# Three weight loads of a fused state-space and gated feed-forward kernel moved to other places in their DMA queues

## The chip, the cores and the metric

The kernel runs on one core of one Trainium2 chip. The metric is the device time of one execution in microseconds (us), the median of several runs. One further execution was recorded by the hardware profiler, and its trace is what the views below answer from. Times inside it count from the start of the span, the first recorded instruction to the last.

The engines are called PE (TensorE, matmul), PEld (its weight loads), DVE (VectorE), ACT (ScalarE), POOL (GpSimd) and SP (SyncE). A name with a q behind it (SPq, ACTq) is that engine's instruction queue issuing a DMA.

## The reference

```
xn = layernorm(x)                                     # x: 2048 tokens x 512
# A: diagonal complex state-space layer, 512 states
Bu = xn @ B_bar.T                                     # B_bar from B_re, B_im, Lambda, dt
h[t] = Lam_bar * h[t-1] + Bu[t]                       # complex scan over the 2048 tokens
yA = 2 * Re(h @ C.T) + xn * Dskip                     # C = C_re + i C_im
# B: gated feed-forward, 1376 hidden columns
yB = (silu(xn @ w_gate) * (xn @ w_up)) @ w_down
out = x + yA + yB                                     # bf16
```

## The kernel before

The 2048 tokens go in four chunks of 512. Everything on TensorE is a matmul with 512 moving columns, four of them (one for each 128 of the 512 inputs) into one PSUM bank. For each chunk there is a B projection (`bproj_tile`, 8 tiles: 4 groups of states for the real and 4 for the imaginary part, L370), a gate/up pass (`gateup_tile`: 10 full column blocks of gate and of up, L445, and a mixed last block, L503) and later the output matmuls. ScalarE takes each bank out of PSUM (L372 for the B projection, L464 and L465 for gate and up, L506 and L507 for the last block). VectorE makes the rotations, scans and products of the state-space part. There are 8 PSUM banks, given out in turn by one pool.

The instructions of each engine stand in the order in which the Python code emits them. VectorE work comes out of a backlog, a few pieces after each group of matmuls (`pump`). The order around the change is

1. gate/up columns 0 to 6 of chunk 0, for which the weights came in groups 0 to 2,
2. the B projection of chunk 0, first the four real tiles, then the four imaginary ones,
3. the rest of chunk 0's gate/up pass: blocks 7 to 9 from group 3 (384 columns of `w_gate` in `wg_g[3]`, 384 of `w_up` in `wu_g[3]`), and the last block from `w_last`,
4. the B projection of chunk 1, then its gate/up pass, and so on.

The loads are issued by hand. SP's queue carries the token tiles (`xall`), the weight groups, the transposed loads of `B_re` and `B_im` into `BT` (four DMA transposes each, L138), the transposes of the normalized tokens of chunk 1 (L249, one for each 128 tokens), then by `load_late` the tokens of chunks 2 and 3 (L156) and `w_down` in two halves (`wd_sb`, L159), and then the eight transposed loads of `C_re` and `C_im` (`CT`, L862). `load_mid` is called before step 1, `load_late` just before step 3.

`wu_last` is a small tile: the last block's first 64 up columns. It is loaded from ScalarE's queue (L155) at the head of `load_late`, and is used by `up_halves` (L492), after chunk 0's output matmuls.

A DMA that SP or ScalarE issues tells of its landing through one of eight semaphores, which the framework gives to these DMAs in turn, in the order in which the code issues them. A DMA whose semaphore is still in use by an earlier one is issued only after that one has landed: the wait stands in the instruction stream of the engine that issues it.

Of the kernel before, what the change touches and what calls it, by code (L numbers as in the profile page):

```python
# [23 lines left out]
def kernel(  # L24
# [17 lines left out]
    nc = tc.nc  # L42
# [9 lines left out]
    KD = D // 128  # L52
    HK = KD // 2
# [6 lines left out]
    LA, LB = 32, 64  # L60
    FL = (FT - 1) * 128
# [20 lines left out]
    wg_v = B_w_gate.rearrange("(k p) f -> p k f", p=128)  # L82
    wu_v = B_w_up.rearrange("(k p) f -> p k f", p=128)
# [6 lines left out]
    wg_g, wu_g = [], []  # L90
# [5 lines left out]
    wu_last = const.tile([128, KD, LB], BF16, name="wu_last")  # L96
# [14 lines left out]
    def load_w1(q, tiles, view, gi):  # L111
        a, b = fgroups[gi]
        q.dma_start(out=tiles[gi][:], in_=view[:, :, a * 128:min(F, b * 128)])
# [23 lines left out]
    def load_bt(part, k):  # L137
        nc.sync.dma_start_transpose(out=BT[:, part, k, :], in_=(A_B_re, A_B_im)[part][:, k * 128:(k + 1) * 128])  # L138
# [4 lines left out]
    def load_mid():  # L143
        nc.sync.dma_start(out=xall[:, TPC:2 * TPC, :], in_=x_v[:, TPC:2 * TPC, :])
        for k in range(HK, KD):
            load_bt(0, k)
        for k in range(KD):
            load_bt(1, k)
        load_w1(nc.sync, wg_g, wg_v, 3)
        load_w1(nc.sync, wu_g, wu_v, 3)  # L150
        nc.sync.dma_start(out=w_last[:, :, 0:LB + LA], in_=wg_v[:, :, FL:F])
        nc.sync.dma_start(out=w_last[:, :, LB + LA:128], in_=wu_v[:, :, FL + LB:F])

    def load_late():
        nc.scalar.dma_start(out=wu_last[:], in_=wu_v[:, :, FL:FL + LB])  # L155
        nc.sync.dma_start(out=xall[:, 2 * TPC:NT, :], in_=x_v[:, 2 * TPC:NT, :])  # L156
        wd_v = B_w_down[0:FL, :].rearrange("(k p) d -> p k d", p=128)
        for a, b in ((0, FT // 2), (FT // 2, FT - 1)):
            nc.sync.dma_start(out=wd_sb[:, a:b, :], in_=wd_v[:, a:b, :])  # L159
# [351 lines left out]
    def gateup_tile(c, fi):  # L511
        if fi == FT - 1:
            return gateup_last(c)
        psg = bank()
        gu_mm(psg, wg_g, c, fi, 0, CW)
        psu = bank()
        gu_mm(psu, wu_g, c, fi, 0, CW)
        gu_out(c, fi, psg, psu)
# [113 lines left out]
    def pump(us):  # L632

        owed[0] += us
        while backlog and owed[0] >= backlog[0][0] * 0.5:
            step()
        if not backlog:
            owed[0] = 0.0

    def multiply(keep):  # L640

        while len(products) > keep:
            products.pop(0)()
            owed[0] -= 0.65
# [75 lines left out]
    norm_dve(3)  # L720
    xT_dma(3)
    load_mid()
    head_mm(0, 2, 3, range(0, HK), range(H))
    head_mm(1, 2, 3, range(0, HK), range(H))
# [116 lines left out]
    for part in range(2):  # L841
        for q in range(NQ):
# [10 lines left out]
           ["ln2"] * len(norm2) + ["ln3"] * (len(stats3) + len(norm3)))  # L853
    queue("cf", c_ops())
    load_late()
    for fi in range(G0, FT):
        gateup_tile(0, fi)
        pump(GU)
        multiply(1)
    for part, src in enumerate((A_C_re, A_C_im)):  # L860
        for q in range(NQ):
            nc.sync.dma_start_transpose(out=CT[:, part, q, :], in_=src[:, q * 128:(q + 1) * 128])  # L862
# [50 lines left out]
```

## Time and profile before

| | |
|---|---|
| median of 3 runs | 178.35 us (178.32 to 178.7) |
| the profiled execution's own time | 178.76 us |
| its span | 177.0 us |
| PE busy | 173.5 us, 98% |
| DVE busy | 153.9 us, 87% |
| ACT busy | 95.3 us, 54% |
| DMA queue of SP (q1) | 11.51 MB, 27.3% of 16 engines' span |
| DMA queue of ACT (q10) | 0.62 MB, 1.7% |

In the views, a line of the chain or the timeline starts with the start time and the duration in us. For a DMA in a queue's timeline, this duration is the time that the issue takes in the queue, not the transfer. A line of DMA issues ends with the time in us from the issue to the landing. "x4" means four instructions in one line.

### The profile page before, as it was taken

How to read it: one execution, taken by the hardware profiler on the slowest of the kernel's cores; microseconds unless marked ns; L12 is line 12 of the kernel's file. 1: busy time of each engine (PE TensorE's matmuls, PEld its weight loads, DVE VectorE, ACT ScalarE, POOL GpSimd, SP SyncE). 2: the span in 40 equal slices, each digit the busy share in tenths (PEclk: the TensorE clock that was granted, in tenths of full speed). 3: DMA queues.
4: the chain of work that ended last, by engine and by line, in shares of the span. 5: the costliest groups of instructions: out<-in, count | busy, mean ns of one | idle time of the engine just before them, and what ended most of it. 6: DMA issues, size and time to landing. Idle time of an engine off the chain costs nothing.

```text
span 177.0 us, 2607 instructions
## 1 busy us (share of the span) xinstructions
PE 173.5 (98%) x955; PEld 84.1 (48%) x955; DVE 153.9 (87%) x233; ACT 95.3 (54%) x174; POOL 51.8 (29%) x86
## 2 busy tenths in 40 slices
PE   8999999999999999999999999999999999999993
PEld 2977644444444444444444444444444444444443
DVE  3779999999999997999999999999999999971033
ACT  3477898867797679613666661053866610001300
POOL 6050120002300210029997040058476500001410
PEclk9999999999999999999999999999999999999999
DMA  5998497996440014900000020019699200000652
GB/s 169 306 167 204 91 257 80 305 305 129 89 87 6 0 36 82 355 5 17 17 19 17 0 82 11 0 20 129 88 147 189 46 2 0 0 4 0 63 98 76
DMA packets 31292, 16.36 MB, mean 92 GB/s; under 512 B 20208, under 2 KB 31088, under 8 KB 31248
## 3 DMA queue, kind: packets, MB, share of 16 engines
q1 hardware_dynamic: 24704, 11.51, 27.3%
q0 software_dynamic: 5184, 4.07, 15.9%
q10 hardware_dynamic: 1392, 0.62, 1.7%
q8 instruction: 7, 0.11, 0.3%
q14 instruction: 5, 0.04, 0.1%
HBM read 8.33 MB, written 5.24 MB: 77 GB/s over the span
## 4 chain that ended last, share of the span: by engine, by line
PE 98%; DVE 0%; issue 0%
PE ps L445 35%; PE ps L594 16%; PE ps L370 16%; PE ps L556 10%; PE ps L582 10%; PE ps L683 2%; PE ps L660 2%; PE ps L503 2%; PE ps L759 2%; PE ps L545 2%; PE ps L492 1%; PE ps L235 1%; DVE res L599 0%; PE ps L265 0%
## 5 line engine op out<-in xcount | busy, mean ns | idle before, releaser
L445 PE MATMUL ps<-xnT,wg 128*128 128x512 bf16 (+1 forms) x148 | 36.6, 373 | 0.0
L445 PE MATMUL ps<-xnT,wu 128*128 128x512 bf16 (+1 forms) x148 | 36.6, 373 | 0.0
L412 DVE TENSOR_TENSOR_SCAN g<-r_t,car,u 128x512 bf16<-128x512 f32 x24 | 28.8, 1263 | 0.0
L370 PE MATMUL ps<-xnT,BT 128*128 128x512 bf16 x128 | 28.3, 379 | 0.0
L594 PE MATMUL ps<-CF,wt 128*128 128x512 bf16 (+2 forms) x144 | 28.2, 356 | 0.0
L464 ACT ACTIVATE guT<-ps 128x512 bf16<-128x512 f32 (+1 forms) x40 | 23.5, 587 | 6.7 <-PE ps L445 6.0
L465 ACT CAST u<-ps 128x512 bf16<-128x512 f32 (+1 forms) x40 | 23.0, 575 | 6.9 <-PE ps L445 6.6
L607 ACT CAST res<-ps 128x512 bf16<-128x512 f32 x12 | 6.7, 590 | 36.0 <-PE ps L594 26.8
L445 PEld LDWEIGHTS <-wu 128*128 128x128 bf16 x148 | 14.5, 98 | 16.6
L187 POOL DMA_DIRECT2D gu_rows<-ul x36 | 17.6, 499 | 15.8 <-DVE ul L480 15.8
L445 PEld LDWEIGHTS <-wg 128*128 128x128 bf16 x148 | 14.4, 98 | 16.5
L608 POOL DMA_DIRECT2D out_dram<-res x12 | 10.5, 1220 | 37.4 <-ACT res L607 37.2
L372 ACT CAST u<-ps 128x512 bf16<-128x512 f32 x32 | 18.2, 586 | 6.0 <-PE ps L370 5.9
L594 PEld LDWEIGHTS <-wt 128*128 128x128 bf16 x144 | 13.3, 98 | 15.0 <-issue 1.3
L370 PEld LDWEIGHTS <-BT 128*128 128x128 bf16 x128 | 12.5, 98 | 14.8
L212 POOL TENSOR_TENSOR rstd<-ve,neg_half 128x2 f32<-128x2 f32 (+1 forms) x4 | 5.7, 1418 | 44.4 <-DVE ve L211 44.4
L582 PE MATMUL ps<-wd_sb,guT 128*128 128x512 bf16 x80 | 17.6, 379 | 0.0
L556 PE MATMUL ps<-wd_sb,guT 128*128 128x512 bf16 x80 | 17.4, 379 | 0.0
L460 DVE TENSOR_TENSOR guT<-guT,u 128x1024 bf16<-128x1024 bf16 x20 | 13.4, 677 | 0.0
L582 PEld LDWEIGHTS <-guT 128*128 128x128 bf16 x80 | 7.8, 98 | 9.4
L556 PEld LDWEIGHTS <-guT 128*128 128x128 bf16 x80 | 7.8, 98 | 9.4
L203 DVE BATCH_NORM_STATS2 stats<-xall 128x6 f32<-128x512 bf16 x14 | 9.5, 679 | 1.9 <-DMA xall<-in_A_x_dram 1.8
(120 smaller groups left out, 200.8 us busy)
## 6 DMA issues: line engine op xcount, KB each, us to landing
out_dram<-in_A_x_dram SPq DMA_DIRECT2D x1, 1536.0 KB, 6.8
out_dram<-res POOLq DMA_DIRECT2D x12, 128.0 KB, 3.6
out_dram<-xall POOLq DMA_DIRECT2D x3, 512.0 KB, 7.4
wd_sb<-in_B_w_down_dram SPq DMA_DIRECT2D x2, 640.0 KB, 7.7
xall<-in_A_x_dram SPq DMA_DIRECT2D x1, 1024.0 KB, 5.9
gu_rows<-ul POOLq DMA_DIRECT2D x36, 8.0 KB, 1.6
wg<-in_B_w_gate_dram SPq DMA_DIRECT2D x1, 512.0 KB, 5.0
wu<-in_B_w_up_dram SPq DMA_DIRECT2D x1, 512.0 KB, 6.0
```

The costliest lines, as they stand in the source:

```text
L187: nc.gpsimd.dma_start(out=gu_rows[c][i * RT:(i + 1) * RT, p, :], in_=product[p * RT:(p + 1) * RT, i * 128:(i + 1) * 128])
L370: nc.tensor.matmul(ps[:], lhsT=BT[:, part, k, q * 128:(q + 1) * 128], rhs=xnT[:, k, c * CW:(c + 1) * CW], start=(k == 0), stop=(k == KD - 1))
L372: nc.scalar.copy(out=u_tiles[c][:, part, q, :], in_=ps[:])
L412: V.tensor_tensor_scan(out=g()[:, part, q, :], data0=r_t[:, q:q + 1].to_broadcast([128, CW]), data1=u_tiles[c][:, part, q, :], initial=ini ...
L445: nc.tensor.matmul(ps[:fs, lo:hi], lhsT=wslice(groups, fi, k), rhs=xnT[:, k, c * CW + lo:c * CW + hi], start=(k == 0), stop=(k == KD - 1))
L460: products.append(lambda: V.tensor_tensor(out=g, in0=g, in1=u, op=ALU.mult))
L464: nc.scalar.activation(out=gu_tile(c)[:, fi, 0:hi], in_=psg[:, 0:hi], func=ACT.Silu)
L465: nc.scalar.copy(out=u_tile(c, fi)[:, fi % 2, 0:hi], in_=psu[:, 0:hi])
L556: nc.tensor.matmul(o[:], lhsT=gu_tiles[k][:, fi, i * 128:(i + 1) * 128], rhs=wd_sb[:, fi, :], start=(fi == 0), stop=False)
L582: nc.tensor.matmul(o[:], lhsT=gu_tiles[c][:, fi, i * 128:(i + 1) * 128], rhs=wd_sb[:, fi, lo:hi], start=(fi == 0), stop=False)
L594: nc.tensor.matmul(o, lhsT=w_tiles[c][:, part, q, i * 128:(i + 1) * 128], rhs=CF[:, part, q, lo:hi], start=(fresh and part == 0 and q == 0 ...
L608: nc.gpsimd.dma_start(out=out_v[:, n, :], in_=res[:], accum_op=ALU.add)
```

## The change

The gate weights' last group is issued between the second and the third imaginary B transpose, where it stood behind the fourth. The up weights' last group stays behind the fourth. The load of `wu_last` goes from the head of `load_late`, ahead of the remaining gate/up blocks of chunk 0, to behind them. It stays in ScalarE's queue. No arithmetic is changed, and each engine's compute instructions keep their order.

```diff
@@ load_mid
         for k in range(HK, KD):
             load_bt(0, k)
-        for k in range(KD):
-            load_bt(1, k)
-        load_w1(nc.sync, wg_g, wg_v, 3)
-        load_w1(nc.sync, wu_g, wu_v, 3)
+        for groups, view, ks in ((wg_g, wg_v, range(0, HK)), (wu_g, wu_v, range(HK, KD))):
+            for k in ks:
+                load_bt(1, k)
+            load_w1(nc.sync, groups, view, 3)
         nc.sync.dma_start(out=w_last[:, :, 0:LB + LA], in_=wg_v[:, :, FL:F])
         nc.sync.dma_start(out=w_last[:, :, LB + LA:128], in_=wu_v[:, :, FL + LB:F])
 
     def load_late():
-        nc.scalar.dma_start(out=wu_last[:], in_=wu_v[:, :, FL:FL + LB])
         nc.sync.dma_start(out=xall[:, 2 * TPC:NT, :], in_=x_v[:, 2 * TPC:NT, :])
...
@@ behind load_late()
     for fi in range(G0, FT):
         gateup_tile(0, fi)
         pump(GU)
         multiply(1)
+    nc.scalar.dma_start(out=wu_last[:], in_=wu_v[:, :, FL:FL + LB])
     for part, src in enumerate((A_C_re, A_C_im)):
         for q in range(NQ):
             nc.sync.dma_start_transpose(out=CT[:, part, q, :], in_=src[:, q * 128:(q + 1) * 128])
```

## The prediction

> **What bounds the kernel now.** I read the page first, then the chain of waits in order of time, then the queues of SP and ACT around the moved loads.
>
> ```profile
> PE 173.5 (98%) x955; PEld 84.1 (48%) x955; DVE 153.9 (87%) x233; ACT 95.3 (54%) x174; POOL 51.8 (29%) x86
> ...
> 25.92 5.18 PE ps L445 x24
> 31.10 0.86 PE ps L503 x4
> 31.96 6.91 PE ps L370 x32
> 38.87 0.86 PE ps L503 x4
> ...
> 174.27 0.02 issue
> 174.29 0.29 DVE res L599
> ```
>
> TensorE bounds everything. The chain is a row of matmul groups without a hole: 24 gate/up matmuls take 5.18 us (0.216 each), the 32 of chunk 1's B projection 6.91 (0.216 each). So no load that the change moves is waited for now, and there is nothing to gain where they are used: if the first gate matmul of the last group waited, the 25.92 line would be longer than 24 x 0.216 = 5.18. On the other side PE has no slack, so any hole that the change makes is paid in full at the end. The whole question is whether it makes one.
>
> **The gate group between the transposes.** Rows of SP's queue and of landings, before:
>
> ```profile
> 10.97 0.59 SPq L144 DMA_DIRECT2D xall<-in_A_x_dram  x1
> 11.60 1.75 SPq L138 DMA_TRANSPOSE BT<-in_A_B_re_dram  x1
> 13.39 1.27 SPq L138 DMA_TRANSPOSE BT<-in_A_B_re_dram  x1
> 17.32 1.26 SPq L138 DMA_TRANSPOSE BT<-in_A_B_im_dram  x1
> 18.62 1.26 SPq L138 DMA_TRANSPOSE BT<-in_A_B_im_dram  x1
> 19.93 0.58 SPq L113 DMA_DIRECT2D wg<-in_B_w_gate_dram  x1
> ...
> xall<-in_A_x_dram SPq DMA_DIRECT2D x1, 512.0 KB, 4.4
> BT<-in_A_B_re_dram SPq DMA_TRANSPOSE x1, 4.2
> BT<-in_A_B_re_dram SPq DMA_TRANSPOSE x1, 3.5
> BT<-in_A_B_im_dram SPq DMA_TRANSPOSE x1, 2.7
> wg<-in_B_w_gate_dram SPq DMA_DIRECT2D x1, 384.0 KB, 4.0
> ...
> 18.85 7.07 PE L370 MATMUL ps<-xnT,BT 128*128 128x512 bf16 x32
> ```
>
> The fourth imaginary transpose is issued at 18.62 and lands 2.7 later, at 21.3. It is the weight of the 20th matmul of chunk 0's B projection, which starts at 18.85 + 19 x 0.216 = 22.95: 1.6 us of slack. After the change the gate group takes the slot at 17.32, and the third and fourth transposes queue behind it. The trace has this pattern once: 512 KB of `xall` issued at 10.97 landed at 15.4, the transpose behind it (its issue stretched to 1.75) landed 4.2 after 11.60, at 15.8, and the next one 3.5 after 13.39, at 16.9. So the two land 0.4 and 1.5 behind the copy. The gate group, landing 4.0 after 17.32, is there at 21.3, the third transpose at 21.7 (its matmul starts at 22.74) and the fourth at 22.8, for a need at 22.95. By the same pattern the fourth is issued at 17.32 + 0.62 + 1.79 = 19.73 and with 2.7 lands at 22.4, with 3.5 at 23.2. I take no stall; the bounds are 0 and 0.3 us. What hides a small stall is the larger one below: a PE that is late at 23 has as much less to wait at 39.
>
> The issues behind are pushed by about half a microsecond, to an end of 22.7, still ahead of the next transpose at 23.14, so SP's later work does not move from this. The up group keeps its place. No gain anywhere: nothing waited for these groups.
>
> **`wu_last` out of the way of SP's queue.** Here the move does something:
>
> ```profile
> 23.14 1.22 SPq L249 DMA_TRANSPOSE xnT<-xall  x1
> 24.45 1.21 SPq L249 DMA_TRANSPOSE xnT<-xall  x1
> 25.76 2.48 SPq L249 DMA_TRANSPOSE xnT<-xall  x1
> 28.32 1.29 SPq L249 DMA_TRANSPOSE xnT<-xall  x1
> 29.67 0.57 SPq L156 DMA_DIRECT2D xall<-in_A_x_dram  x1
> 30.91 0.68 SPq L159 DMA_DIRECT2D wd_sb<-in_B_w_down_dram  x1
> ...
> 27.50:28.50 1.00, 1.00 (x6) 0.48 (x5) 0.91 (x2) 0.81 (x2) 0.00 (x0) 1.00 1.49 34
> ...
> q10 hardware_dynamic: 53, 0.01, 80.7%
> ...
> wd_sb<-in_B_w_down_dram SPq DMA_DIRECT2D x1, 640.0 KB, 8.3
> ```
>
> The four transposes of chunk 1 are issued back to back. Three take 1.21 to 1.29 us, the third takes 2.48, and it is the one beside which ACT issues `wu_last` (25.97, below). In the stage 27.5 to 28.5 the DMA engines are counted as full (1.49, the two queues on top of each other) and move 34 GB/s; 80.7% of it is 53 packets of q10, ACT's queue, which is `wu_last`. The small load and the transposes block each other. With `wu_last` gone from there, the third issue should take 1.22, and all behind it on SP comes 2.48 - 1.22 = 1.26 us earlier: the second half of `w_down` is issued at 29.65 instead of 30.91. It landed at 30.91 + 8.3 = 39.2; now at 37.95. By itself this gives nothing, since PE waits for none of these.
>
> **`wu_last` in its new place.** In the built program its issue stands in ACT's stream right behind the two evictions of the last block, ahead of the eight of chunk 1's B projection, and it has the semaphore that the second `w_down` half uses just before it:
>
> ```
> SP   30  DMACopy wd_sb<-in_B_w_down_dram 128x5x512     [waits DMAHW6]
> ACT  44  TensorCopy ul<-ps 32x512
> ACT  45  DMACopy wu_last<-in_B_w_up_dram 128x4x64      [waits DMAHW6]
> ```
>
> SP 30 waits for the third count of this semaphore and makes the fourth; ACT 45 waits for the fourth, so for the landing of `w_down`. Before, it waited for `w_last`, which had landed by then. This is an added wait, and queued behind it on ACT are all evictions of PSUM.
>
> ```profile
> 24.32 2.23 ACT L372 CAST u<-ps 128x512 bf16<-128x512 f32 x4
> 25.97 0.41 ACTq L155 DMA_DIRECT2D wu_last<-in_B_w_up_dram  x1
> ...
> 32.61 0.58 ACT L507 CAST ul<-ps 32x512 bf16<-32x512 f32 x1
> 33.21 1.11 ACT L372 CAST u<-ps 128x512 bf16<-128x512 f32 x2
> ...
> 38.71 1.03 PE L503 MATMUL ps<-xnT,w_last 128*128 128x512 bf16 x4
> ...
> 45.54 0.81 ACT L225 ACTIVATE xall<-xall,nb,rstd 128x512 bf16<-128x512 bf16 x1 [1.73 <-DVE nb L215]
> ...
> 138.75 2.45 POOL L187 DMA_DIRECT2D gu_rows<-gu_last  x5 [2.26 <-DMA out_dram<-xall]
> ```
>
> That an issue held back for an earlier landing stops its engine's stream is what the POOL line shows: 2.26 us idle ahead of five small DMAs, ended by the landing of a store. ACT reaches its new wait at 32.61 + 0.58 = 33.2 and stands until 37.95. Meanwhile PE goes on: bank by bank the eight tiles of chunk 1's B projection fill all 8 banks, the last being the one that L507 released at 33.2. The next bank needed is the first tile's, for the last block of chunk 1, now started at 38.71. It comes free when ACT has issued the DMA (0.41, the 25.97 line) and copied that tile (0.58, as the L507 line and the L372 lines): 37.95 + 0.41 + 0.58 = 38.94. Three hand-overs (landing to issue, issue to copy, copy to matmul) add some 0.05 each, by the gaps between SP's issues (23.14 + 1.22 to 24.45 is 0.09): 39.09. **PE waits 39.09 - 38.71 = 0.38 us.** Bounds: without hand-overs and a landing 0.25 earlier, 0; with a landing 0.4 later, 0.8.
>
> [...] Had the wait sat in the DMA queue, ACT would pass it and the sum would be 0.
>
> After that ACT has eight tiles to catch up, about 0.48 each when they lie ready (two in 1.11 us, with the second's own 0.58, are at most 0.53 apart), against 0.86 us of PE for each bank. It reaches chunk 1's second gate/up pair at about 45.3, where it idled 1.73 us before 45.54, so the lag is gone and no second hole follows. DVE's products of chunk 1 come after that.
>
> The load itself now runs beside the `CT` transposes, which it may slow by the same 1.3 us; neither is needed soon:
>
> ```profile
> L353 ACT ACTIVATE cm<-CT,c2re x4: 715/716/734, 65.7 to 70.8; 128x512 f32<-128x512 bf16 x4
> L492 PE MATMUL ps<-xnT,wu_last x16: 379/379/403, 72.5 to 74.0; 128*64 128x512 bf16 x16
> ```
>
> **Sum.** 0 for the groups, 0 for SP's relief by itself, +0.38 for the hole near 38.9. The profiled execution goes from a span of 177.0 to 177.38 and from 178.76 to 179.14; against the median, which is 0.41 below that execution, 178.35 + 0.38, about **178.75 us**. A difference of 0.2% (0.36 us) is about what a measurement of this kernel can tell from no change, so the forecast lies close to that line.
>
> **Rivals.**
>
> *SP's relief doesn't come, or only in part.* If the third transpose's 2.48 us has another cause (the loads in flight ahead of it), `w_down` lands at 39.2 as before, the first tile's bank is free at 39.2 + 0.99 + 0.15 = 40.34, and PE waits 1.63: 179.98 us. For it: other issues right behind large copies were stretched too (the 1.75 at 11.60). Against: here no large copy was issued just before, two transposes in between took 1.22 and 1.21, and the q10 row names the culprit. A partial form: the DMA engines gave `wu_last` some 0.8 x 1 us between 27.5 and 28.5; if the transposes got only half of it back, the hole is about 1.2, 179.6 us. [...] Chance of this rival 0.14.
>
> *The fourth imaginary transpose is late by more than the hole hides.* From a landing of 23.4 on, the stall at 23 exceeds 0.4 and sets the end; at 0.5 beyond the bound of 23.2, it would be 0.75: 179.1 us. For it: the slack of 1.6 shrinks to 0.15. Against: the gate group is a quarter smaller than the copy of the pattern. Chance 0.05.
>
> *No hole, and a little faster.* From a landing of 37.55 on, 0.4 earlier than worked out, ACT's wait is covered by the eight banks, and PE never stops. What then can be gained is what PE loses elsewhere; `wu_last`'s first matmuls at 72.5 have one of 403 ns against 379, so some hundredths: 178.3 us. To gain over 0.2% the work outside PE's chain (0.8 us ahead of it, 2.7 behind 174.27) would have to shrink, which nothing in the change touches. Chance of a gain over 0.2%: 0.03.
>
> **How the numbers follow.** The forecast (a hole of 0 to 0.9 at 39) has 0.76; a little over half of it, 0.42, lies above 0.36, the rest, 0.34, below. Slower by over 0.2%: 0.42 + 0.14 + 0.05 = 0.61. Faster: 0.03. Within 0.2%: 0.36, with 0.02 for what I have not named. The range goes from no hole (178.3) to the first rival in full (180.0).
>
> **What would show it.** In the profile after: the chain of waits has a hole, or an ACT copy of L371, between the B projection of chunk 1 and its last block; SP's third chunk-1 transpose takes about 1.2; `w_down`'s second half is issued near 29.65; ACT idles from 33.2 for about 5 us and ends it by a DMA. I am wrong if ACT's evictions go on through 33 to 38, if the third transpose still takes 2.5, or if PE stands near 23.

## The result, and the profile after

The changed kernel takes 179.58 us (median of 6 runs, 179.25 to 180.01) against 178.33 us for the kernel before (6 runs, 178.23 to 178.7): slower by 1.25 us, ratio 1.0071 with a 95% interval of 1.0054 to 1.0087. It was forecast slower at 178.75, in a range of 178.3 to 180.0. The direction and the added wait came as forecast; the size is over three times the +0.38 of the sum. The trace below is of an execution of 180.01 us, the longest of the six.

The chain of waits after (start, duration, what; compute lines of after stand one lower than before, L371 is the eviction of the B projection that was L372) is no longer PE alone:

```profile
27.68 0.85 SPq L248
28.58 0.57 SPq L155
29.21 0.57 SPq L158
29.82 8.98 DMA wd_sb<-in_B_w_down_dram
38.83 0.41 ACTq L859
39.28 0.59 ACT u L371
39.91 1.02 PE ps L502 x4
40.94 17.27 PE ps L444 x80
...
175.49 0.29 DVE res L598
```

It is to be read upwards from 39.91: the last block of chunk 1 (L502) waited for an eviction, the eviction for ACT's issue of `wu_last` (L859), and the issue for the landing of the second `w_down` half, which SP had issued at 29.82. From there on PE runs without a hole, as before.

ACT's timeline shows the stop from the other side, and the list of waits gives it a name:

```profile
32.01 0.58 ACT L506 CAST ul<-ps 32x512 bf16<-32x512 f32 x1
38.83 0.41 ACTq L859 DMA_DIRECT2D wu_last<-in_B_w_up_dram  x1
39.28 4.01 ACT L371 CAST u<-ps 128x512 bf16<-128x512 f32 x8 [6.69 <-DMA wd_sb<-in_B_w_down_dram]
...
46.29 0.84 ACT L224 ACTIVATE xall<-xall,nb,rstd 128x512 bf16<-128x512 bf16 x1
...
54.79 0.59 ACT L464 CAST u<-ps 128x512 bf16<-128x512 f32 x1 [0.19 <-PE ps L444]
...
31.21 7.07 PE L369 MATMUL ps<-xnT,BT 128*128 128x512 bf16 x32
39.91 1.02 PE L502 MATMUL ps<-xnT,w_last 128*128 128x512 bf16 x4 [1.64 <-ACT u L371]
```

ACT computes nothing for 6.69 us, then makes the eight evictions of the B projection in one go (4.01 us, about 0.5 each). It waits for PE again only at 54.79; until then it works without a pause. PE's wait is 1.64 us by this view.

That is more than the 1.2 us by which the profiled span grew (177.0 to 178.2), because in this execution PE had come to the B projection of chunk 0 earlier:

```profile
18.26 7.07 PE L369 MATMUL ps<-xnT,BT 128*128 128x512 bf16 x32
```

It was 18.85 before, 0.59 later. The view counts PE's wait from the modelled end of the last matmul, which overlaps the start of the next. From start to start the delay is 39.91 - (31.21 + 6.91) = 1.79 us, with 6.91 us for 32 matmuls, and 1.79 - 0.59 = 1.20. In the changed kernel most of such a lead is lost, since the landing sets the time at which PE goes on: a second profile of it, further down, has PE there at 18.88 and a span only 0.2 longer. From the restart to the end of the span it is 178.2 - 39.91 = 138.3 us; before, from the same matmul, 177.0 - 38.71 = 138.3. So the span after is the landing, plus 1.11 us to PE's restart, plus 138.3, and the price of the change is the restart at 39.91 against the 38.71 of before: 1.20.

### The profile page after: what moved, and what is told of

Its sections match the earlier page's. It is cut to its first block, busy times and chain, and to the rows that moved or that the text cites. A ratio compares the mean times of both kernels' runs of the same rounds, so it can differ in the third digit from the quotient of the medians.

```text
span 178.2 us, 2607 instructions
## 1 busy us (share of the span) xinstructions
PE 173.0 (97%) x955; PEld 83.5 (47%) x955; DVE 153.8 (86%) x233; ACT 94.4 (53%) x174; POOL 51.9 (29%) x86
## 3 DMA queue, kind: packets, MB, share of 16 engines
q1 hardware_dynamic: 24704, 11.51, 27.6%
q10 hardware_dynamic: 1392, 0.62, 1.2%
## 4 chain that ended last, share of the span: by engine, by line
PE 80%; DVE 10%; DMA 5%; SPq 1%; issue 1%; POOL 1%; ACT 0%; ACTq 0%; DVEq 0%; POOLq 0%
PE ps L444 29%; PE ps L593 16%; PE ps L555 10%; PE ps L581 10%; PE ps L369 8%; DMA wd_sb<-in_B_w_down_dram 5%; PE ps L659 2%; DVE pm L304 2%; PE ps L544 2%; PE ps L502 2%; DVE pm L303 2%; DVE stats L202 1%; PE ps L682 1%; PE ps L491 1%; DVE guT L459 1%; DVE pm L295 1%
## 5 line engine op out<-in xcount | busy, mean ns | idle before, releaser
L593 PE MATMUL ps<-CF,wt 128*128 128x512 bf16 (+2 forms) x144 | 28.2, 356 | 0.0
L371 ACT CAST u<-ps 128x512 bf16<-128x512 f32 x32 | 17.7, 598 | 11.0 <-DMA wd_sb<-in_B_w_down_dram 6.7
L607 POOL DMA_DIRECT2D out_dram<-res x12 | 10.6, 1223 | 37.7 <-ACT res L606 37.6
```

The costliest lines, as they stand in the source:

```text
L371: nc.scalar.copy(out=u_tiles[c][:, part, q, :], in_=ps[:])
L593: nc.tensor.matmul(o, lhsT=w_tiles[c][:, part, q, i * 128:(i + 1) * 128], rhs=CF[:, part, q, lo:hi], start=(fresh and part == 0 and q == 0 ...
```

## The experiments

The theory: ACT stands at the moved issue until `w_down`'s second half has landed, and PE runs out of free banks; all of the loss is there. The rivals: the gate group between the transposes costs the time, or the small load does, by its place or traffic, whatever it waits for. Each kernel below was timed against runs of the kernel before on the same chip (178.46 us for the first four, 178.41 for the next four).

**One part of the change at a time.** The change moves two loads, the gate group (by which two B transposes go later) and `wu_last`. First only the move of `wu_last`:

```diff
     def load_late():
-        nc.scalar.dma_start(out=wu_last[:], in_=wu_v[:, :, FL:FL + LB])
...
         multiply(1)
+    nc.scalar.dma_start(out=wu_last[:], in_=wu_v[:, :, FL:FL + LB])
```

> Only the load of wu_last is moved; the gate group stays behind the four imaginary transposes. Theory (ACT stands at the moved issue until the second w_down half has landed, and PE runs out of banks): the whole loss of the changed kernel, about 179.5 us (179.2 to 180.0), with a hole of 1 to 2 us in PE at 39 to 40, ended by an eviction of the B projection. Rival (the gate group between the transposes costs the time): no loss, 178.35 us within 0.2%, no hole.

Measured: 179.81 us, ratio 1.0075 (1.0052 to 1.0098), the whole loss. The hole is the same, from the chain:

```profile
29.25 9.49 DMA wd_sb<-in_B_w_down_dram
38.76 0.41 ACTq L859
39.21 0.59 ACT u L371
39.85 1.02 PE ps L502 x4
```

Then only the order of the groups and transposes:

```diff
-        for k in range(KD):
-            load_bt(1, k)
-        load_w1(nc.sync, wg_g, wg_v, 3)
-        load_w1(nc.sync, wu_g, wu_v, 3)
+        for groups, view, ks in ((wg_g, wg_v, range(0, HK)), (wu_g, wu_v, range(HK, KD))):
+            for k in ks:
+                load_bt(1, k)
+            load_w1(nc.sync, groups, view, 3)
```

> Only the gate group is moved; wu_last is loaded at the head of load_late as before. Theory: 178.35 us within 0.2% or at most 0.3 us above, with a PE wait of 0 to 0.3 us for the fourth imaginary transpose at 22 to 23 and no hole at 39. Rival (the gate group costs the time): 179.5 us.

Measured: 178.47 us, ratio 1.0 (0.9989 to 1.0011). No hole. The first rival is out: the gate group costs nothing that can be measured.

**The same place, another semaphore.** The issue stays where the change put it. The `C` loads are issued later, behind the transposes of chunk 2's tokens; by that the framework's turn gives `wu_last` a semaphore whose last user landed long before.

```diff
-    for part, src in enumerate((A_C_re, A_C_im)):
-        for q in range(NQ):
-            nc.sync.dma_start_transpose(out=CT[:, part, q, :], in_=src[:, q * 128:(q + 1) * 128])
...
-    gateup_chunk(1)
+    for j, fi in enumerate([FT - 1, *range(FT - 1)]):
+        if j == 6:
...
+        gateup_tile(1, fi)
+        pump(GU)
+        multiply(1)
```

> The changed kernel, with wu_last issued at the same place of ACT's stream, but the C loads are issued later, behind the transposes of chunk 2's tokens; by that the framework gives wu_last the semaphore that the second w_last load used, which has landed at 25 to 26. Theory (it is the wait for w_down's landing): no stop of ACT beyond the issue's 0.41 us, no hole at 39; 178.35 us, with up to 0.3 more for the fourth imaginary transpose. Rival (the load at this place costs by itself, by its issue on ACT or by its traffic): 179.5 us as the changed kernel.

Measured: 178.43 us, ratio 0.9998 (0.9987 to 1.0009). ACT's timeline at the place of the stop:

```profile
31.58 0.59 ACT L505 ACTIVATE gu_last<-ps 96x512 bf16<-96x512 f32 x1
31.59 0.39 ACTq L859 DMA_DIRECT2D wu_last<-in_B_w_up_dram  x1
32.19 0.58 ACT L506 CAST ul<-ps 32x512 bf16<-32x512 f32 x1
32.79 1.10 ACT L371 CAST u<-ps 128x512 bf16<-128x512 f32 x2
```

The issue goes out beside the evictions and they follow one another. `w_down` itself lands no sooner by much: issued at 29.24, 9.3 us later, at 38.5. So neither the place nor the load costs; the wait does. This also corrects a statement made ahead of the prediction: the semaphores' turn does not follow the order of the code. In the changed kernel `wu_last` stands ahead of the `C` loads in the code, yet it got its semaphore as if behind seven of the eight, and so the one of `w_down` (DMAHW6, of DMAHW0 to DMAHW7 in the built program).

**A stop that the banks cover.** The issue is put one block earlier:

```diff
     for fi in range(G0, FT):
+        if fi == 10:
+            nc.scalar.dma_start(out=wu_last[:], in_=wu_v[:, :, FL:FL + LB])
         gateup_tile(0, fi)
         pump(GU)
         multiply(1)
-    nc.scalar.dma_start(out=wu_last[:], in_=wu_v[:, :, FL:FL + LB])
```

> The changed kernel, with wu_last issued one block earlier, ahead of the last gate/up block of chunk 0. There its semaphore's last user is the load of the tokens of chunks 2 and 3, which landed at 35.2 in the changed kernel. Theory (a stop of ACT costs only what the free PSUM banks don't cover): ACT stands from about 31.4 to 35.2, almost 4 us, then needs 0.41 + 3 x 0.6 for the issue, two evictions of the last block; the bank of that block is wanted by the 8th B projection tile at 38.0 and is free by 37: no hole, 178.35 us, up to 0.3 more. Rival (any stop of ACT of several us is paid in full or in part): 179.3 to 180 us.

Measured: 178.43 us, ratio 0.9993 (0.9983 to 1.0003).

```profile
35.05 0.45 ACTq L857 DMA_DIRECT2D wu_last<-in_B_w_up_dram  x1
35.55 0.59 ACT L505 ACTIVATE gu_last<-ps 96x512 bf16<-96x512 f32 x1 [3.48 <-PE ps L369]
...
31.92 6.91 PE ps L369 x32
38.83 0.86 PE ps L502 x4
```

ACT stands here too, 3.48 us, and PE passes without a hole (the last two lines are its chain). The view puts ACT's idle time down to PE, which came last among what that eviction waited for; the ACTq line ahead of it shows what ended it. This stop of ACT cost nothing because the issue and the evictions behind it were done before PE wanted the next bank: the last block's was free at 36.15 + 0.58 = 36.73 for the eighth tile at 31.92 + 28 x 0.216 = 37.97, the first tile's at 36.75 + 0.59 = 37.34 for 38.83. In the changed kernel, where the bank that PE wants needs one eviction, that way back takes about 1.1 us.

**Less and more ahead of the landing.** With 512 KB fewer ahead of `w_down`:

```diff
-        nc.sync.dma_start(out=xall[:, 2 * TPC:NT, :], in_=x_v[:, 2 * TPC:NT, :])
+        nc.sync.dma_start(out=xall[:, 2 * TPC:3 * TPC, :], in_=x_v[:, 2 * TPC:3 * TPC, :])
...
-    gateup_chunk(1)
+    for j, fi in enumerate([FT - 1, *range(FT - 1)]):
+        if j == 3:
+            nc.gpsimd.dma_start(out=xall[:, 3 * TPC:NT, :], in_=x_v[:, 3 * TPC:NT, :])
+        gateup_tile(1, fi)
+        pump(GU)
+        multiply(1)
```

> The changed kernel, with the 512 KB of chunk 3's tokens taken out of the large load ahead of w_down and loaded later from POOL's queue. By the framework's turn wu_last on ACT now waits for the first C transpose, which lands 0.5 us behind w_down (38.80 and 39.29 in the changed kernel). Theory with landing set by the bytes ahead (640 KB took 1.75 us between the landings of the two halves): both land 1.4 us earlier, ACT goes on at 37.9, the first tile's bank is free at 39.0 instead of 39.9: a loss of 0.3 us against before instead of 1.25, 178.7 us (178.4 to 179.1). If the landing doesn't follow the bytes: 179.6 to 180.1, as the semaphore's user lands later than w_down. Rival (the place or the small load itself costs): 179.6.

Measured: 178.52 us, ratio 1.0005 (0.9991 to 1.0018).

```profile
wd_sb<-in_B_w_down_dram SPq DMA_DIRECT2D x1, 640.0 KB, 6.7
...
37.46 0.45 ACTq L859 DMA_DIRECT2D wu_last<-in_B_w_up_dram  x1
37.95 4.01 ACT L371 CAST u<-ps 128x512 bf16<-128x512 f32 x8 [4.97 <-PE ps L369]
...
38.58 1.02 PE L502 MATMUL ps<-xnT,w_last 128*128 128x512 bf16 x4
```

With fewer bytes ahead `w_down` lands 6.7 us after its issue instead of 8.98, and the first `C` transpose, for which ACT waits here, right behind it. ACT goes on at 37.46, and PE's restart at 38.58 falls within 0.1 us of where the bank is wanted. The landing that ACT waits for comes 1.4 us earlier (37.4 against 38.8), and the hole is gone. The margin is thin: one of the 11 executions took 179.47 us, and as it has no trace, it is not known whether its landing came late.

With 512 KB of on-chip copying beside `w_down`:

```diff
+    nc.gpsimd.dma_start(out=CF[:, 0, :, :], in_=c16[:])
     nc.scalar.dma_start(out=wu_last[:], in_=wu_v[:, :, FL:FL + LB])
```

> The changed kernel with 512 KB of additional traffic: POOL's queue copies a finished table on the chip into a tile that is only written much later, from 31 to 32 us on, beside the w_down loads. Nothing waits for it soon. Theory: w_down's second half lands up to 1.4 us later (half of the engines' time goes to the copy while it lasts), ACT stands as much longer, PE's hole grows by as much: 180.3 to 181.1 us. Rival (the loss doesn't hang on w_down's landing): 179.6 as the changed kernel.

Measured: 181.48 us, ratio 1.0175 (1.0141 to 1.0209), above what was expected in the median (180.68 to 182.91 over six runs).

```profile
29.88 10.16 DMA wd_sb<-in_B_w_down_dram
40.06 0.41 ACTq L860
40.51 0.59 ACT u L371
41.15 1.02 PE ps L502 x4
```

The landing came 1.2 us later than in the changed kernel, the restart 41.15 - 39.91 = 1.24 later, and the span grew from 178.2 to 179.5. The half share of the engines' time that was expected for the copy was the author's estimate; no view here shows the share. Last, the same traffic in the version with the free semaphore:

> The same additional 512 KB of traffic in the version with wu_last at the same place of ACT's stream and a semaphore that is free (the C loads issued later). Theory: w_down lands later as well, but nobody waits for it: 178.4 us (178.2 to 178.7). Rival (the added traffic costs by itself): above 179.

Measured: 178.36 us, ratio 0.9997 (0.9987 to 1.0008). There `w_down` was issued at 29.80 and landed 10.6 us later, at 40.4, and nobody waited for it. So the traffic costs only through the wait.

**Another queue.** The changed kernel with `nc.sync` in place of `nc.scalar` for `wu_last`:

> The changed kernel, with wu_last issued from SP's queue behind the two w_down halves instead of ACT's. The order of loads on the chip stays about the same; no eviction stands behind the issue. Theory: no hole, 178.4 us (178.2 to 178.7), the same as before, since PE bounds before and after alike. Rival (the late place of wu_last or its traffic costs): 179.3 to 179.6 us.

Measured: 178.56 us, ratio 1.0012 (1.0002 to 1.0021). The hole is gone.

```profile
30.19 1.93 SPq L859 DMA_DIRECT2D wu_last<-in_B_w_up_dram  x1
...
wd_sb<-in_B_w_down_dram SPq DMA_DIRECT2D x1, 640.0 KB, 8.2
```

The second `w_down` half was issued at 29.62 and landed at 37.85, but SP issued `wu_last` at 30.19 already. So the framework's turn had given it another semaphore here too, and nothing waited for that landing. The run shows that the late load costs next to nothing from SP's queue; it does not separate the queue from the semaphore. Whether the 0.1% that is left is real, at the edge of its interval, the profile doesn't say: it has no hole in PE at 39.

**Both kernels once more**, for a second profile each.

> The kernel before, unchanged, for a second profile. If the 2.48 us issue of the third transpose of chunk 1 was made by wu_last on ACT's queue, it is there again (2.3 to 2.6); if it is chance, it takes 1.2 or anything up to 2.5. w_down's second half: issued at 29.2 to 30.9, landing at 38.5 to 39.3 whatever the issue, if the landing doesn't follow the issue.

The kernel before, SP's queue:

```profile
25.33 1.22 SPq L249 DMA_TRANSPOSE xnT<-xall  x1
...
30.11 0.52 SPq L159 DMA_DIRECT2D wd_sb<-in_B_w_down_dram  x1
...
wd_sb<-in_B_w_down_dram SPq DMA_DIRECT2D x1, 640.0 KB, 8.7
...
25.55 0.41 ACTq L155 DMA_DIRECT2D wu_last<-in_B_w_up_dram  x1
```

With `wu_last` issued beside it, the third transpose took 1.22 us this time, not 2.48.

> The changed kernel, unchanged, for a second profile. Theory: again one hole in PE ahead of the last block of chunk 1, its end 1.05 to 1.15 us behind w_down's landing (issue 0.41, eviction 0.59, hand-overs); the landing at 38.5 to 39.4; so a span of 177.5 to 178.6. The third transpose's issue: 1.2 if wu_last made it long before, up to 2.5 if it is chance.

The changed kernel, SP's third transpose and the chain:

```profile
25.80 2.06 SPq L248 DMA_TRANSPOSE xnT<-xall  x1
...
30.46 8.58 DMA wd_sb<-in_B_w_down_dram
39.06 0.40 ACTq L859
39.51 0.59 ACT u L371
40.14 1.02 PE ps L502 x4
```

Without `wu_last` near it took 2.06. The span was 178.4, and 40.14 + 138.3 is 178.4 again.

## Why the prediction was right or wrong

**The added wait** was right in its place, its cause and its consequences. ACT's stop was forecast from 33.2 on, ended by `w_down`'s landing; it came from 32.6 on, in an execution 0.6 ahead. From the landing to PE's restart 1.14 us were summed (0.41 + 0.58 + three hand-overs). The chains have 1.11 in the changed kernel (29.82 + 8.98 = 38.80, to 39.91), 1.11 (38.74 to 39.85), 1.10 (39.04 to 40.14) and 1.11 (40.04 to 41.15). That the eight banks cover PE until chunk 1's last block, and that no second hole follows, is what the trace after shows. ACT's lag lasted longer than forecast, though: it was to be gone at about 45.3, and ACT first waits for PE again at 54.79.

**The step that failed is SP's relief**, the 1.26 us by which the landing was to come earlier: 37.95 was forecast, 38.80 and 39.04 were measured. It failed twice over.

First, the third transpose is stretched without `wu_last`, and not always with it. With the load beside it, it took 2.48 in one profile of before, but 1.22 in the other and in the run with the gate group alone. Without it, it took 1.94 to 2.13 in six profiles, those of the changed kernel with 2.05 and 2.06 among them, and 1.22 in three. The row of 27.5 to 28.5 was misread as well. 80.7% is ACT's queue's share of the engines' time, not of what they were busy with, and SP's queue has nearly as much:

```profile
q10 hardware_dynamic: 53, 0.01, 80.7%
q1 hardware_dynamic: 109, 0.03, 68.2%
```

By these rows a packet took 0.24 us in ACT's queue and 0.10 in SP's in that microsecond (0.807 x 16 / 53 and 0.682 x 16 / 109), against 0.03 in either over the whole span (1392 packets in 1.7% of 16 x 177 us, 24704 in 27.3%). The packets of both queues were held up, and the row doesn't say which held which, or whether a third thing held both. There is a third thing in the trace. Queue q8, listed as `instruction`, moves 16 KB in one packet. In the window from 25.7 to 28.2 it has one packet in every profile but that of the run with `wu_last` moved alone; this is its row before:

```profile
q8 instruction: 1, 0.02, 3.4%
```

In ten profiles that packet starts between 25.8 and 26.6, and in each of them the third transpose is stretched or else the fourth (to 1.30, 1.49 and 1.54). In the second profile of before it comes at 27.8, and in the run with `wu_last` moved alone at 34.9. In these two all four transposes took 1.21 or 1.22, and what SP issued beside the packet took longer instead:

```profile
27.91 1.53 SPq L156 DMA_DIRECT2D xall<-in_A_x_dram  x1
34.73 2.72 SPq L862 DMA_TRANSPOSE CT<-in_A_C_re_dram  x1
```

In the first profile of before these two took 0.57 and 1.42. Not every long issue has such a packet beside it: the first `C` transpose, right behind the large loads, took 4.04 in the changed kernel without one. No run moved this instruction load, so this is a coincidence in all twelve profiles and not a shown cause; what makes the stretch stays open.

Secondly, and this weighs more, the landing follows the issue poorly. Nine profiles have the same 2.3 MB in the queue and no added copy. In order of the issue of the second half, it landed

| issued | 29.24 | 29.25 | 29.62 | 29.82 | 29.90 | 30.11 | 30.41 | 30.46 | 30.91 |
|---|---|---|---|---|---|---|---|---|---|
| landed | 38.6 | 38.7 | 37.85 | 38.8 | 39.3 | 38.8 | 38.7 | 39.0 | 39.2 |

The issues differ by up to 1.67 us, the landings by 1.4, and in no clear order. A landing near the forecast 37.95 did occur once, in the run with `wu_last` on SP's queue. But in the two profiles in which none of the four transposes was stretched, and another issue was instead, it came at 38.7 and 38.8. So the 1.26 was not to be counted on. What does move the landing is the traffic, as the runs with less and more of it show: the one that ACT waits for came 1.4 us earlier with 512 KB fewer ahead, 1.2 later with 512 KB of copying beside. Why an earlier issue brings so little was not settled.

With a landing near 38.8 the restart is near 39.9, against 38.71 in the first profile of before: +1.2, and 178.35 + 1.2 = 179.55. This is the partial form of the first rival ("in part", 179.6), with another reason than it gave. The forecast had it at 0.14 together with the full form; the weight went to the likelier-looking reading of one profile. Of the six executions after, the middle span is 177.8; if 1.11 and 138.3 hold there too, its landing was at 38.4 (an estimate).

**The gate group** was right: no cost by the run with it alone. The fourth imaginary transpose, forecast to land at 22.8 by the clock of before, was issued at 19.04 and landed 3.1 later, at 22.1, in an execution in which PE was 0.6 ahead; that is 22.7 by that clock. The second profile of after shows the small stall that the prediction allowed for: there the transpose landed 3.5 after 19.51, at 23.0, about when its matmul was due (18.88 + 19 x 0.216 = 22.98), and chunk 0's B projection took 7.19 us instead of 7.07. That 0.1 us lies within the bounds of 0 to 0.3 and was hidden by the wait at 39, in the way the prediction described. The second rival, a stall larger than that wait hides, did not occur.

**The bounds** of 0 to 0.8 for the hole were too narrow, because both were worked out from the one landing time that the relief gave. The range held because the rival in full was its upper end, and not by the sum; to that extent it was luck.

That an issue held back for an earlier landing stops its engine's stream, which the prediction read from POOL's 2.26 us, holds for ACT in the trace after: the 6.69 us of ACT's idle time are put down to the landing, and ACT's issue at 38.83 follows that landing at 38.80.

## What to carry to other kernels

In this kernel a DMA issued from the engine that also frees the PSUM banks stopped that engine for 6.69 us, until an unrelated earlier DMA with the same completion semaphore had landed; with a semaphore whose last user had landed, the same issue at the same place stopped nothing. So look up in the built program whose semaphore an issue gets, and when its last user lands, before moving it. The price was the time until the landing plus the way back to the first free bank, minus the time that the free banks cover: 3.48 us of standing cost nothing here, 6.69 us cost 1.20. Before a gain is booked on a stretched instruction, see whether it is stretched in a second profile, and whether what comes behind it is bound by its issue or by the bytes ahead of it.

## What the runs showed of the hardware that was not expected

The issue of one and the same DMA transpose took 1.22 us in some executions and 1.94 to 2.48 in others; the kernel before has both 1.22 and 2.48. The last 640 KB of 2.3 MB in one queue landed between 37.85 and 39.3 us in the nine profiles listed above, with little regard to their issue between 29.24 and 30.91. And the start of chunk 0's B projection on PE differs by 0.4 to 0.6 us between executions of one kernel: 18.85 and 18.41 before, 18.26 and 18.88 after.

```profile
18.41 7.07 PE L370 MATMUL ps<-xnT,BT 128*128 128x512 bf16 x31
18.88 7.19 PE L369 MATMUL ps<-xnT,BT 128*128 128x512 bf16 x31
41.15 1.02 PE L502 MATMUL ps<-xnT,w_last 128*128 128x512 bf16 x4 [2.78 <-ACT u L371]
core 0: 179.5 us, clock 1.000
```

The first two lines are the second profiles of before and after; the last two belong to the run with more traffic, PE's hole and the granted clock. The mean clock stayed at 1.000 with a hole of 2.78 us, the longest that a traced execution had here. One execution of the run with more traffic took 182.91 us at a mean clock of 0.991, the lowest here; it has no trace, so what lowered its clock, and how long its hole was, is not known.
